# Spectral rows for the inverse transform gathered one token block at a time instead of eight

## The chip, the core and the metric

The kernel runs on one core of a Trainium2 chip. A core has five engines that work side by side, each through its own queue in the order in which the instructions were written into it: PE (TensorE, matrix multiplication into PSUM; the profile counts its weight loads apart, as PEld), DVE (VectorE), ACT (ScalarE), POOL (GpSimd) and SP (SyncE, which here only issues DMAs). SBUF is the working memory, PSUM holds what PE accumulates. The metric is the device time of one execution in microseconds (us), lower is better. Shapes are given as partitions x elements per partition.

## The reference

The input x has 2048 tokens of 448 features (f32). With LN for a layer normalisation over the features, the reference computes

```
xn  = LN(x)
A   = irfft2(rfft2(xn, axes=(token, feature)) * (w_r + 1j*w_i))
h   = gelu(LN(xn) @ w1); quarters of the features shifted by +1, -1, +2, -2 tokens
x1  = xn + shifted(h) @ w2
B   = x1 + gelu(LN(x1) @ w3) @ w4
out = x + A + B
```

w1 and w2 are 448 x 448, w3 is 448 x 1792, w4 is 1792 x 448, and w_r and w_i are 2048 x 225. The spectral branch A has four steps that matter here: a real transform over features and over part of the tokens, a transform over the rest of the tokens, the product with the weights, and the way back. The change lies at the beginning of the way back.

## The kernel before

**Tiling.** Token number 16a + b is row a of block b, so there are 16 blocks of 128 tokens, one token per partition; xb(b) is the f32 tile part of block b in xt. It first holds the normalised input, then everything that is added to it. Every f32 operand of a matmul is split into two f16 parts, high and low, and each product is made of three passes (high x high, high x low, low x high), the tuple PASS in the code.

**Stages in the order of the program.** Loads, the first normalisation, w1, the shifts and w2 (`w1_unit`, `w2_tile`); the second normalisation (`ln2`); the MLP with w3 and w4 for pairs of blocks, G = 0 to 7, each in seven steps fp (`front` makes 256 hidden features of a pair and their gelu, `back` multiplies them with w4); beside it the forward transform (`step1`) and, for 16 chunks of frequencies c, the spectral product (`chunk_a`, `chunk_b`, `chunk_z`, `chunk_c`); last the inverse stage for 16 blocks (`gather_u`, `inv_a`, `inv_b`, `finish`).

**Around the change.** `chunk_c` writes, for one chunk c, both f16 parts of its spectral rows into Y (L641 on ACT, L642 on DVE). Y is one tile of [128, 2 parts, 4 families q, 16 chunks c, 128]; the view Y1 reads the last 128 as 16 blocks b of 8 rows k. An inverse matmul for block b needs, as its weights, 128 columns: the 8 rows k of all 16 chunks c. In Y these stand in 16 runs of 8 elements, 128 elements apart. `gather_u` copies them on DVE (L651) into a tile U in which they are contiguous. As every block needs a row of every chunk, no gather can begin before the last `chunk_c` is through.

`gather_u(b0)` takes eight blocks at a time: two tiles (high and low part) of [128, 4, 8, 128] f16, one buffer each, and eight copies of 113 x 1024 elements, one for each part and each q. The first call serves blocks 8 to 15, the second blocks 0 to 7. The second writes the same two buffers and so waits until all inverse matmuls of the first eight blocks have read them.

`inv_a(b)` then runs 12 matmuls of 113 columns (L659) into a PSUM bank pe (tag "tr", two banks), copies it out with a scale on ACT (L663), folds it with two additions on POOL (L666, L667) and four additions and subtractions on DVE (L668 to L671) into v, and splits v into vh (L673 on ACT, L674 on DVE). The work tile of L663 to L671 alternates between two stage buffers; vh has two. `inv_b(b)` runs three matmuls of 448 columns (L681) into a PSUM bank py (tag "sp", two banks), and adds the result to xb(b) on DVE (L682). `finish(b)` loads the block's original x into one of two rows xr, adds xb(b) to it (L493 on DVE) and stores it. Blocks are taken in the order 12 to 15, 8 to 11, 0 to 7. Blocks 12 to 15 are finished later, in the MLP of the last two pairs.

**What sets the order.** Nothing here is ordered by hand. A planner simulates the engines with durations of its own and writes each engine's queue beforehand, taking among the instructions that are ready the one of the best priority. Priorities follow the order of the program, with two exceptions: the MLP's matmuls (`front` L381, `back` L716) have the priority FILL, below everything else, and what empties their PSUM banks (the gelu L694 and the split L696 on ACT, L697 on DVE, and the additions L728 and L723 on DVE) has EVAC, above everything else. So the matmuls of the MLP fill PE where the spectral branch leaves it free. `mlp(range(3, 6))` stands ahead of the inverse stage in the program, and `mlp(range(6, 8), last=True)` behind it. Both add to xb(b), and additions to one xb(b) keep the order of the program.

Of the kernel before, what the change touches and what calls it, by code (L numbers as in the profile page):

```python
# [13 lines left out]
F16 = mybir.dt.float16  # L14
# [6 lines left out]
NB, NC = 16, 16  # L21
# [98 lines left out]
def body(tc, nc, x, wf, w1, w2, w3, w4, c_g, c_n, c_small, out):  # L120
    V, A, P, T, SY = nc.vector, nc.scalar, nc.gpsimd, nc.tensor, nc.sync
# [13 lines left out]
    def pool(name, bufs=1, side="left", space=None):  # L135
        kw = dict(name=name, bufs=bufs, reuse_waits="tile")
        if space is not None:
            kw["space"] = space
        else:
            kw["side"] = side  # L140
        cm = tc.tile_pool(**kw)
        opened[name] = cm
        return cm.__enter__()
# [6 lines left out]
    def bank(tag, name):  # L150
        return ps.tile([128, 512], F32, tag=tag, bufs=2, name=name)
# [16 lines left out]
    def stage(name, n, side, dtype=F32):  # L168
        t = pw.tile([128, 1808], F32, tag=f"stage{side}", bufs=1, name=name)
        return (t if dtype is F32 else t.bitcast(dtype))[:, :n]  # L170
# [325 lines left out]
    def finish(b):  # L496
        SY.dma_start(ov[:, b], unscaled(b))
# [146 lines left out]

    U, vhs = {}, {}

    def gather_u(b0):
        U[b0] = [pv.tile([128, 4, 8, 128], F16, tag=f"U{p}", bufs=1, name=f"U{b0}{p}") for p in range(2)]
        for p in range(2):
            for q in range(4):  # L650
                V.tensor_copy(out=U[b0][p][:113, q].rearrange("p b (c k) -> p b c k", c=NC),  # L651
                              in_=Y1[:113, p, q, :, b0:b0 + 8].rearrange("p c b k -> p b c k"))

    def inv_a(b):
        pe = bank("tr", f"pe{b}")
        for q in range(4):
            kd = 113 - q // 2
            for n, (ui, ii) in enumerate(PASS):
                T.matmul(pe[:, 113 * q:113 * q + 113], U[b // 8 * 8][ui][:kd, q, b % 8, :],  # L659
                         cI[ii][:kd, 113 * q:113 * q + 113], start=n == 0, stop=n == 2)  # L660
        w = stage(f"e{b}", 1808, b % 2)
        e, v = w[:, 0:452], w[:, 904:904 + D]
        A.activation(out=e, in_=pe[:, :452], func=AF.Copy, scale=VPRE)  # L663
        u = w[:, 452:904].rearrange("p (a b d) -> p a b d", a=2, b=2)
        uf = u.rearrange("p a b d -> p a (b d)")
        P.tensor_tensor(out=uf[:, 0], in0=e[:, 0:226], in1=e[:, 226:452], op=ALU.add)  # L666
        P.tensor_tensor(out=uf[:, 1], in0=e[:, 0:226], in1=e[:, 226:452], op=ALU.subtract)  # L667
        V.tensor_tensor(out=v[:, 0:113], in0=u[:, 0, 0], in1=u[:, 0, 1], op=ALU.add)  # L668
        V.tensor_tensor(out=v[:, 447:335:-1], in0=u[:, 0, 0, 1:113], in1=u[:, 0, 1, 1:113], op=ALU.subtract)
        V.tensor_tensor(out=v[:, 224:112:-1], in0=u[:, 1, 0, 0:112], in1=u[:, 1, 1, 0:112], op=ALU.subtract)  # L670
        V.tensor_tensor(out=v[:, 225:336], in0=u[:, 1, 0, 1:112], in1=u[:, 1, 1, 1:112], op=ALU.add)  # L671
        vh = pv.tile([128, 2, D], F16, tag="vh", bufs=2, name=f"vh{b}")
        A.activation(out=vh[:, 0], in_=v, func=AF.Copy)  # L673
        V.tensor_tensor(out=vh[:, 1], in0=v, in1=vh[:, 0], op=ALU.subtract)  # L674
        vhs[b] = vh

    def inv_b(b):
        vh = vhs.pop(b)
        py = bank("sp", f"py{b}")
        for n, (vi, ri) in enumerate(PASS):  # L680
            T.matmul(py[:, :D], cV[ri], vh[:, vi], start=n == 0, stop=n == 2)  # L681
        V.scalar_tensor_tensor(out=xb(b), in0=py[:, :D], scalar=sc[:, 1:2], in1=xb(b), op0=ALU.mult, op1=ALU.add)  # L682
# [209 lines left out]
    Y1 = Y.rearrange("p i q c (b k) -> p i q c b k", k=8)  # L892
# [33 lines left out]
    pv = pool("pv", side="right")  # L926
    bs = [*range(12, 16), *range(8, 12), *range(8)]
    for n in range(17):
        if n in (0, 8):
            gather_u(8 - n)  # L930
        if n < 16:
            inv_a(bs[n])
        if n:
            b = bs[n - 1]
            inv_b(b)
            if b < 12:
                finish(b)
# [27 lines left out]
```

## Time and profile before

| | |
|---|---|
| time, median of 3 runs | 420.48 us (420.2 to 420.87) |
| the profiled execution's own time | 420.4 us |
| busy: PEld | 291.7 us |
| busy: DVE | 291.6 us |
| busy: ACT | 248.1 us |
| busy: POOL | 118.6 us |
| first and last copy of a gather begin at | 286.2 and 312.5 us |
| first and last inverse matmul (L659) begin at | 289.3 and 355.0 us |
| DMA, whole span | 47.61 MB |

The profile is that of one execution; times in it count from the start of its span. A row of the timeline gives start, duration, engine, line, operation, output <- inputs, shape, and the number of instructions merged into it; in square brackets stands for how long the engine had been idle before it and which instruction ended that wait. A row of a window view gives the stretch, its length, an engine's busy time with the number of its instructions, the granted clock of PE as a share of full speed, and two figures for DMA. "PEld" rows are weight loads, which run beside matmuls. The end of a matmul is modelled, and consecutive ones overlap, so their spacing is read from their starts.

### The profile page before, as it was taken

What the parts mean: (1) busy time and instruction counts of PE and PEld (TensorE: products, weight loads), DVE (VectorE), ACT (ScalarE), POOL (GpSimd) and SP (SyncE); (2) the same over time, 40 slices, a digit from 0 to 9 for tenths busy, and PEclk for the clock granted to TensorE, in tenths of its full rate; (3) what the DMA queues carried; (4) which work ended last, traced back from release to release, by engine and by line L of the source; (5) the groups of instructions that cost most, each with busy time, mean ns of one, the idle gap of its engine ahead of it and who ended that gap; (6) DMA issues with size and microseconds to landing.
All of it is one profiled execution on the core that took longest, in us unless ns stands there. A gap on an engine that the chain in (4) does not pass through costs nothing.

```text
span 418.6 us, 8535 instructions
## 1 busy us (share of the span) xinstructions
PE 409.8 (98%) x3329; PEld 291.7 (70%) x3329; DVE 291.6 (70%) x615; ACT 248.1 (59%) x428; POOL 118.6 (28%) x204
## 2 busy tenths in 40 slices
PE   7999999999999999999999999999999999999996
PEld 3655555765668777776887887777776767577785
DVE  4888899798774766652689889865999529942112
ACT  4698869972758866632678888864534414422331
POOL 3876700101345746300031221211454203200000
DMA  8959982734761365315056555610001003331001
GB/s 271 362 174 175 275 174 95 132 78 90 191 156 50 89 234 165 93 41 140 14 142 173 149 144 142 177 39 2 2 2 68 22 2 132 134 133 40 5 0 45
DMA packets 51832, 47.61 MB, mean 114 GB/s; under 512 B 33936, under 2 KB 47056, under 8 KB 51792
## 3 DMA queue, kind: packets, MB, share of 16 engines
q1 hardware_dynamic: 51792, 47.07, 41.7%
q8 instruction: 26, 0.43, 0.4%
q14 instruction: 14, 0.11, 0.1%
HBM read 35.52 MB, written 3.67 MB: 94 GB/s over the span
## 4 chain that ended last, share of the span: by engine, by line
PE 72%; DVE 14%; DMA 6%; issue 5%; POOL 1%; ACT 1%; SPq 1%; POOLq 0%; DVEq 0%
PE pw L381 25%; PE acc L716 22%; PE pw L450 7%; PE pw L410 6%; PE ps L536 3%; PE pu L638 2%; PE pp L593 2%; PE px L610 2%; DMA xr<-x 1%; DVE w4p L265 1%; DMA out<-xr 1%; PE pta L370 1%; DMA x2mem<-y 1%; DVE xt L682 1%; DVE sta L289 1%
## 5 line engine op out<-in xcount | busy, mean ns | idle before, releaser
L381 PE MATMUL pw<-x2mem,w3p 128*128 128x256 f16 x1232 | 151.8, 273 | 0.0
L716 PE MATMUL acc<-w4p,hf 128*128 128x448 f16 (+1 forms) x714 | 140.0, 341 | 0.7 <-DVE hf L697 0.7
L381 PEld LDWEIGHTS <-w3p 128*128 128x128 f16 x1232 | 118.9, 98 | 23.1 <-issue 0.9
L716 PEld LDWEIGHTS <-hf 128*128 128x128 f16 x714 | 69.2, 98 | 49.2 <-DVE hf L697 1.6
L697 DVE SCALAR_TENSOR_TENSOR hf<-pw,h,hf 128x512 f16<-128x512 f32 x56 | 41.7, 747 | 55.5 <-ACT hf L696 55.3
L694 ACT ACTIVATE pw<-pw,pe 128x512 f32<-128x512 f32 x56 | 36.6, 655 | 70.5 <-PE pw L381 69.4
L450 PE MATMUL pw<-w2p,h 112*128 112x448 f16 x192 | 40.1, 352 | 0.8 <-DMA h<-hs 0.8
L696 ACT ACTIVATE hf<-pw,h 128x512 f16<-128x512 f32 x56 | 38.3, 686 | 1.4
L619 POOL TENSOR_TENSOR z<-te 128x450 f32<-128x450 f32 x16 | 16.3, 1016 | 74.0 <-DVE te L617 74.0
L410 PE MATMUL pw<-w1p,xT 128*128 128x448 f16 x176 | 35.3, 352 | 0.0
L450 PEld LDWEIGHTS <-h 112*128 112x128 f16 x192 | 18.7, 98 | 17.0 <-DMA h<-hs 1.0
L666 POOL TENSOR_TENSOR e<-e 128x226 f32<-128x226 f32 x16 | 13.9, 866 | 56.5 <-ACT e L663 45.3
L410 PEld LDWEIGHTS <-xT 128*128 128x128 f16 x176 | 16.9, 98 | 16.2 <-DVE xT L375 0.8
L600 ACT ACTIVATE pf<-pp 64x450 f16<-64x450 f32 x32 | 17.3, 540 | 16.7 <-DVE pf L601 8.2
L601 DVE TENSOR_TENSOR pf<-pp,pf 64x450 f16<-64x450 f32 x32 | 19.9, 622 | 5.3 <-ACT pf L600 5.0
L663 ACT ACTIVATE e<-pe 128x452 f32<-128x452 f32 x16 | 8.7, 547 | 15.6 <-DVE vh L674 12.3
L516 POOL TENSOR_TENSOR xr<-xf 128x452 f32<-128x452 f32 x8 | 9.7, 1208 | 28.3 <-issue 22.9
L615 ACT ACTIVATE te<-px 64x450 f32<-64x450 f32 x32 | 17.2, 538 | 0.5
L673 ACT ACTIVATE vh<-e 128x448 f16<-128x448 f32 x16 | 9.2, 574 | 14.0 <-DVE e L671 8.3
L519 POOL TENSOR_TENSOR f<-xr 128x452 f32<-128x452 f32 x16 | 16.1, 1028 | 0.6
L527 DVE TENSOR_TENSOR xh<-f,xh 128x452 f16<-128x452 f32 x16 | 11.8, 780 | 5.9 <-ACT xh L526 5.9
L681 PE MATMUL py<-vh,csm 128*128 128x448 f16 x48 | 13.5, 352 | 1.5 <-DVE vh L674 0.7
(163 smaller groups left out, 602.8 us busy)
## 6 DMA issues: line engine op xcount, KB each, us to landing
wc<-wf SPq DMA_DIRECT2D x32, 225.0 KB, 3.7
wl<-wf SPq DMA_DIRECT2D x8, 450.0 KB, 3.7
xt<-x SPq DMA_DIRECT2D x8, 448.0 KB, 8.2
xf<-x SPq DMA_DIRECT2D x8, 448.0 KB, 3.7
w3raw<-w SPq DMA_DIRECT2D x3, 896.0 KB, 12.8
xr<-x SPq DMA_DIRECT2D x12, 224.0 KB, 2.6
out<-xr SPq DMA_DIRECT2D x12, 224.0 KB, 2.0
gn<-c_g SPq DMA_DIRECT2D x16, 128.0 KB, 3.3
```

The costliest lines, as they stand in the source:

```text
L381: T.matmul(ps_out, wp[:, wi + t, cols], xT[:, xi + t, tok], start=t == 0 and wi + xi == 0, stop=t == 3 and wi == 4)
L410: T.matmul(pm[:, :D], xTs[g][:, xi + t, 128 * i:128 * i + 128], w1p[:, wi + t], start=t == 0 and p == 0, stop=t == 3 and p == 2)
L450: T.matmul(pm[:, :D], hT[g][:112, 4 * hi + k, o:o + 128], w2p[:, wi, k], start=n == 0, stop=n == 11)
L519: P.tensor_tensor(out=f[:, :, k:k + 2].rearrange("p b s d -> p s b d"), in0=u[:, :, 0], in1=u[:, :, 1], op=op)
L600: A.activation(out=hi, in_=src, func=AF.Copy)
L601: V.tensor_tensor(out=lo, in0=src, in1=hi, op=ALU.subtract)
L615: A.activation(out=e[64 * h:64 * h + 64], in_=px_[64 - 64 * h:128 - 64 * h, :2 * DF], func=AF.Copy)
L619: P.tensor_tensor(out=z, in0=t[:, 0], in1=t[:, 1], op=ALU.add)
L694: A.activation(out=pm, in_=pm, func=AF.Gelu_apprx_tanh, scale=r3)
L696: i = A.activation(out=h[:, 0], in_=pm, func=AF.Copy, scale=h3)
L697: j = V.scalar_tensor_tensor(out=h[:, 1], in0=pm, scalar=h3, in1=h[:, 0], op0=ALU.mult, op1=ALU.subtract)
L716: m = T.matmul(to, h[:, hi, o:o + 128], w4p[0][:, wi, f, r], start=f == 0 and n == 0, stop=f == 13 and n == 2)
```

## The change

A gather now serves one block. `gather_u(b)` makes one tile U of [128, 2 parts, 4 families, 128] f16, in a ring of four buffers, and fills it with two copies of 113 x 512 elements, one for each part, each over all four families. That is 32 copies in place of 16, with the same elements in all. `inv_a(b)` takes its weights from that tile, with the same shapes as before. In the loop the first two blocks are gathered ahead of the first `inv_a`, and then each time the next block ahead of the present one's `inv_a`. The buffers take 4 x 2 KB per partition in place of 2 x 8 KB.

```diff
-    def gather_u(b0):
-        U[b0] = [pv.tile([128, 4, 8, 128], F16, tag=f"U{p}", bufs=1, name=f"U{b0}{p}") for p in range(2)]
+    def gather_u(b):
+        U[b] = pv.tile([128, 2, 4, 128], F16, tag="U", bufs=4, name=f"U{b}")
         for p in range(2):
-            for q in range(4):
-                V.tensor_copy(out=U[b0][p][:113, q].rearrange("p b (c k) -> p b c k", c=NC),
-                              in_=Y1[:113, p, q, :, b0:b0 + 8].rearrange("p c b k -> p b c k"))
+            V.tensor_copy(out=U[b][:113, p].rearrange("p q (c k) -> p q c k", c=NC), in_=Y1[:113, p, :, :, b])
 
     def inv_a(b):
         pe = bank("tr", f"pe{b}")
+        u = U.pop(b)
         for q in range(4):
             kd = 113 - q // 2
             for n, (ui, ii) in enumerate(PASS):
-                T.matmul(pe[:, 113 * q:113 * q + 113], U[b // 8 * 8][ui][:kd, q, b % 8, :],
+                T.matmul(pe[:, 113 * q:113 * q + 113], u[:kd, ui, q],
                          cI[ii][:kd, 113 * q:113 * q + 113], start=n == 0, stop=n == 2)
@@
     for n in range(17):
-        if n in (0, 8):
-            gather_u(8 - n)
+        if n == 0:
+            gather_u(bs[0])
+        if n < 15:
+            gather_u(bs[n + 1])
         if n < 16:
             inv_a(bs[n])
```

## The prediction

> **What bounds the kernel now.** First the page: its span, and the busy share of each engine. PE is the matrix engine, DVE the vector engine, ACT the scalar engine, POOL the general one.
>
> ```profile
> span 418.6 us, 8535 instructions
> PE 409.8 (98%) x3329; PEld 291.7 (70%) x3329; DVE 291.6 (70%) x615; ACT 248.1 (59%) x428; POOL 118.6 (28%) x204
> ```
>
> PE is busy for 409.8 of 418.6 us. The profiled execution took 420.4 us, so 1.8 us lie around the span, and it stands 0.08 us under the median of 420.48 us. Whatever the change does, it must do it to PE's few idle microseconds, since the matmuls stay the same in number and shape. So the second view is PE's busy time by stretch (stretch, length, busy time, granted clock), from the first gather copy on.
>
> ```profile
> 286.00:331.00 45.00, 43.70 (x406) 1.00 0.06 22
> 345.00:366.00 21.00, 20.47 (x157) 1.00 0.39 132
> 366.00:411.00 45.00, 45.00 (x362) 1.00 0.12 42
> ```
>
> The reader is to see that after 366 us PE is never idle: there only MLP matmuls are left. In the inverse stage the page sees 45.00 - 43.70 = 1.30 and 21.00 - 20.47 = 0.53 us, 1.83 us in all. A matmul's shown end is modelled and overlaps the next, so short gaps hide in busy time. Starts show them. In a stretch of pure MLP work PE's timeline has:
>
> ```profile
> 331.45 2.56 PE L381 MATMUL pw<-x2mem,w3p 128*128 128x256 f16 x22
> 333.85 2.43 PE L716 MATMUL acc<-w4p,hf 128*128 128x448 f16 x12
> 336.12 2.57 PE L381 MATMUL pw<-x2mem,w3p 128*128 128x256 f16 x22
> ```
>
> From start to start, 22 matmuls of 256 columns take 2.40 us, 0.109 each, and 12 of 448 columns take 2.27 us, 0.189 each. By columns, one of 113 takes 113/256 of 0.109, an estimate of 0.048. With these the stall at the second gather is read from the timeline of all engines:
>
> ```profile
> 309.59 3.76 POOL L666 TENSOR_TENSOR e<-e 128x226 f32<-128x226 f32 x1 [3.81 <-ACT e L663]
> ...
> 310.15 2.76 DVE L651 COPY U<-y 113x1024 f16<-113x1024 f16 x8
> ...
> 312.17 1.02 PE L659 MATMUL pe<-csm,U 113*128 113x113 f16 x10
> 312.63 0.17 PEld L659 LDWEIGHTS <-U 112*128 112x128 f16 x3 [0.15 <-DVE U L651]
> ...
> 313.03 1.04 PE L381 MATMUL pw<-x2mem,w3p 128*128 128x256 f16 x8
> ...
> 313.76 1.00 DVE L674 TENSOR_TENSOR vh<-e,vh 128x448 f16<-128x448 f32 x1
> ...
> 314.81 0.35 PE L681 MATMUL py<-vh,csm 128*128 128x448 f16 x1 [0.74 <-DVE vh L674]
> ```
>
> Eight copies hold DVE for 2.76 us. The ten L659 matmuls, which read what the copies write, take 313.03 - 312.17 = 0.86 us where 10 x 0.048 = 0.48 would do: 0.38 us lost, and the weight load names the copy. The eight L381 matmuls then take 314.81 - 313.03 = 1.78 us where 8 x 0.109 = 0.87 would do: 0.91 us lost, until L681 gets its vh from the L674 that stood behind the copies on DVE. So **1.29 us of PE time is lost at the second gather.** The other stall of size is late in the stage:
>
> ```profile
> 361.85 0.54 PE L716 MATMUL acc<-w4p,hf 128*128 128x448 f16 x2
> 362.70 1.12 PE L716 MATMUL acc<-w4p,hf 128*128 128x448 f16 x5 [0.32 <-DVE hf L697]
> 364.04 0.55 PE L681 MATMUL py<-vh,csm 128*128 128x448 f16 x2 [0.21 <-DVE xt L682]
> ```
>
> Here 0.85 - 2 x 0.189 = 0.47 and 1.34 - 5 x 0.189 = 0.39, together 0.86 us, wait for DVE work that is no gather.
>
> **The change part by part.** It removes 16 copies of 1024 elements a partition and adds 32 of 512; no DMA, matmul, ACT or POOL instruction is added or taken, and SP's queue gets nothing new. The copies' price, with the nearest row for one that has no length (a copy of one element), and the group in the stretch of the stage:
>
> ```profile
> L651 DVE COPY U<-y x16: 412/416/422, 286.2 to 312.5; 113x1024 f16<-113x1024 f16 x16
> L565 DVE COPY wt<-wpb x1: 159/159/159, 200.5 to 200.5; 128x1 f32<-128x1 f32 x1
> L651 DVE COPY U<-y 113x1024 f16<-113x1024 f16 x16 | 5.5, 417 | 0.0
> ...
> L668 DVE TENSOR_TENSOR e<-e 128x113 f32<-128x113 f32 x12 | 5.1, 423 | 3.2 <-POOL e L666 3.2
> L671 DVE TENSOR_TENSOR e<-e 128x111 f32<-128x111 f32 x12 | 4.3, 359 | 0.0
> ```
>
> (The first two give minimum, median and maximum in ns; the others total busy us and mean ns.) No copy of 512 elements is in the trace. If nothing of a copy were fixed it would take 208 ns, if everything were, 416. I take the one-element row as the fixed part: 159 + (416 - 159)/2 = 288 ns. Sixteen copies are busy for 5.5 us, 0.344 each, so consecutive ones overlap by 0.07 us. The new ones then hold DVE for 32 x (0.288 - 0.07) = 7.0 us, 1.5 us more than now; the ends are 32 x 0.138 = 4.4 (1.1 us less) and 32 x 0.346 = 11.1 us (5.6 more). [...]
>
> **The first gather.** Now:
>
> ```profile
> 286.18 2.77 DVE L651 COPY U<-y 113x1024 f16<-113x1024 f16 x8
> 288.86 0.75 DVE L697 SCALAR_TENSOR_TENSOR hf<-pw,h,hf 128x512 f16<-128x512 f32 x1
> 291.84 0.64 DVE L668 TENSOR_TENSOR e<-e 128x113 f32<-128x113 f32 x1 [2.23 <-POOL e L666]
> ```
>
> With the change the first block's rows are there after two copies, 2 x 0.22 = 0.44 us, so the first inverse block can start 2.77 - 0.44 = 2.3 us sooner, and the copies of the next three blocks (1.3 us) fit under the 2.23 us for which DVE now waits on POOL. What that gains at the end is **nothing**: PE shows no wait for this burst, MLP matmuls cover it, and what is pulled forward of the inverse pushes as much MLP work behind it. If that cover were gone, it would be worth the 2.3 us. The reason why it cannot be carried on is this pair of DVE's rows:
>
> ```profile
> 344.26 1.44 DVE L728 SCALAR_TENSOR_TENSOR xt<-acc,p,xt 128x448 f32<-128x448 f32 x2 [3.37 <-PE acc L716]
> 345.62 1.27 DVE L682 SCALAR_TENSOR_TENSOR xt<-py,sc,xt 128x448 f32<-128x448 f32 x2
> ```
>
> L682 of blocks 10 and 11 adds to the same xt as L728 of MLP pair 5 and comes after it in the program, so the inverse stops until the third group of MLP work is through, however early it began.
>
> **The second gather** goes: its copies come in pairs, up to three blocks ahead, as ring slots come free. That takes away the 0.38 and the 0.91 us, as far as nothing else makes vh late at that place. Next in line there is the work that stood around the burst on DVE, of 0.6 to 1.0 us an instruction, so I take off the whole 1.29 and keep 0 as the other end.
>
> **The added wait.** Copy n must wait until the 12 L659 matmuls of block n - 4 have read its slot, and behind it on DVE stand L668 to L674, L682 and the MLP's L697, on which PE's L716 waits. Now only the second burst has such a wait, for all eight blocks. A slot is needed again three blocks later, so I price it at nothing; PE's order hides it, and without that cover a pair could cost what the weight load shows at 312.63 us, 0.15 us, 12 times: 1.8 us.
>
> **The copies beside POOL.** At 309.59 us POOL's L666 took 3.76 us, with all eight copies inside. DVE's two-input adds meet POOL too; the first row gives one add over the whole run, the others DVE and POOL in the stretch:
>
> ```profile
> L668 DVE TENSOR_TENSOR e<-e x16: 257/266/656, 291.8 to 362.6; 128x113 f32<-128x113 f32 x16
> 286.00:331.00 45.00, 39.37 (x96) 1.00 0.06 22
> 286.00:331.00 45.00, 18.52 (x24) 1.00 0.06 22
> ```
>
> An undisturbed add takes 0.266 us, the slowest 0.656, so one meeting costs DVE up to 0.39 us. DVE is 39.37/45 = 87% busy and POOL 18.52/45 = 41%. Eight of the new copies fall before POOL has inverse work; if the other 24 meet it by its busy share and wait each time, that is 24 x 0.39 x 0.41 = 3.8 us; with the 1.5 us of fixed parts DVE comes 5.3 us later over the stage, and in the other direction POOL gets its 3.2 us at L666 back. What does DVE's lateness cost PE? L668 and L671 already lose 12 x (0.423 - 0.266) + 12 x (0.359 - 0.266) = 3.0 us to such meetings, and PE's idle time beside the burst is 1.30 - 0.74 = 0.56 us: at most 0.19 us of PE per us of DVE. So the cost lies between 0 and 5.3 x 0.19 = 1.0 us; a DVE that falls fully behind would pass on all of it, which is the rival below. I take the 1.5 us alone, 0.3 us, since POOL's meetings are given back at L666.
>
> [...]
>
> **Sum:** 420.4 - 1.29 + 0.3 = 419.4 us; with the ends of the cost (0 to 1.0) 419.1 to 420.1.
>
> **The rivals.** *Slower: DVE falls behind among POOL's work.* PE takes its instructions in the written order, so if MLP matmuls stand behind L681 and vh is late, PE stands still. For it: DVE is 87% busy, and both stalls shown above are waits for DVE. Against it: 0.19 us per us so far. If half of the 5.3 us reaches PE, it is 420.4 - 1.29 + 2.65 = 421.8 us; if all, 424.4. It is slower than before once more than 1.29/5.3 = 24% of DVE's lateness arrives at PE.
>
> *No difference: the stall moves.* Both the order on PE and that on DVE are laid out anew from the first gather on, since each block's copies are free at other times. Then L681 may wait for vh at another place, as it does at 364.04 us, where no gather is near. The 1.29 us come back elsewhere: 420.4 us.
>
> *Much faster: the early start clears the stage.* With 2.3 us of lead and no gap between blocks 11 and 0, DVE's work is spread and the 0.86 us at 362 us goes too: 420.4 - 1.29 - 0.86 = 418.3 us; and all idle time of the page is 1.83 us, so it can hardly be much more. Against it: the later stretch begins at the same L728 as now.
>
> *The change does not do what it says:* if no slot is free in time, the copies come as late as now, with the 1.8 us of the added wait on top and the 1.29 us kept: 422.2 us. Against it: with four slots the planner may copy three blocks ahead.
>
> **How the numbers follow.** Forecast 0.42, of which 0.30 is faster and 0.12 within the bound (419.4 is only 1.1 us under the median); much faster 0.12; no difference 0.12; slower by DVE's lateness 0.28; slots too late 0.06. A measurement of this kernel can tell about 0.2%, 0.84 us, from no change: faster is under 419.64 us, slower over 421.32. So faster 0.42, same 0.24, slower 0.34. The forecast's own range is 419.1 to 420.1 us. The range for 8 in 10 goes from 418.2, just under the much faster case, to 422.4, over the half-lateness and late-slot cases; the full lateness of 424.4 is left out.
>
> **What would show it.** If the steps are right, the first L659 stands about 2.3 us earlier than its copies now allow; copies come in pairs of about 0.29 us each; no L666 takes over 1.7 us; PE's idle time up to 331 us falls from 1.30 to about 0.5 us, and that after 366 us stays zero. The price is wrong if a copy takes near 0.21 or 0.42 us, the hiding is wrong if weight loads at L659 wait for copies, and the slower rival is right if L651 copies of 0.6 us and more stand ahead of waits of L681 or L716 for DVE. The whole argument is wrong if PE idles after 366 us, or if the instructions ahead of the first gather change place.

## The result and the profile after

The changed kernel takes 421.44 us (median of 16 runs, 421.11 to 421.75), the kernel before 420.56 us (16 runs). The ratio is 1.0023, 95% interval 1.0017 to 1.0030: **slower by 0.9 us** (0.7 to 1.3). 419.4 us and "faster" were forecast.

The page of the changed kernel, and PE's busy time by stretch (stretch, length, busy time, clock, DMA):

```profile
span 419.8 us, 8553 instructions
PE 410.8 (98%) x3329; PEld 291.6 (69%) x3329; DVE 292.6 (70%) x631; ACT 248.1 (59%) x428; POOL 115.5 (28%) x204
```

```profile
286.00:331.00 45.00, 42.79 (x403) 1.00 0.07 22
345.00:366.00 21.00, 20.54 (x156) 1.00 0.40 132
366.00:411.00 45.00, 45.00 (x359) 1.00 0.12 42
```

PE's idle time up to 331 us rose from 1.30 to 2.21 us. These 0.91 us are the whole difference; the later stretch (0.46 in place of 0.53) and the time after 366 us (none) did not move. The profiled pair is 1.2 us apart, but 0.3 us of that lies ahead of the gather: the last L642 begins at 285.89 here and at 285.57 in the kernel before, as in these two rows of the two timelines.

```profile
285.89 0.69 DVE L642 SCALAR_TENSOR_TENSOR y<-pu,y 113x512 f16<-113x512 f32 x1 [1.87 <-ACT y L641]
```

```profile
285.57 0.69 DVE L642 SCALAR_TENSOR_TENSOR y<-pu,y 113x512 f16<-113x512 f32 x1 [1.89 <-ACT y L641]
```

From here on, lines behind 650 have a number one lower in the changed kernel: the copy is L650, the inverse matmuls L658, POOL's additions L665 and L666, the fold L667 to L670, vh L672 and L673, the block's second matmuls L680.

What PE waited for up to 331 us (total, times, longest, in us), in the kernel before and then in the changed one:

```profile
PE py L681 <- DVE vh L674: 0.7, 1, 0.7
PE py L681 <- ACT vh L673: 0.5, 2, 0.3
```

```profile
PE py L680 <- DVE vh L673: 1.0, 1, 1.0
PE py L680 <- ACT vh L672: 0.7, 1, 0.7
PE py L680 <- DVE xt L681: 0.2, 1, 0.2
PE pe L658 <- ACT e L662: 0.2, 1, 0.2
```

Two stalls hold most of the loss, and each stands where the kernel before lost time too. The first, in the timeline of all engines:

```profile
298.76 0.59 POOL L665 TENSOR_TENSOR e<-e 128x226 f32<-128x226 f32 x1 [1.83 <-ACT e L662]
...
298.91 0.57 DVE L669 TENSOR_TENSOR e<-e 128x112 f32<-128x112 f32 x1
299.30 0.62 POOL L666 TENSOR_TENSOR e<-e 128x226 f32<-128x226 f32 x1
...
299.40 0.65 DVE L670 TENSOR_TENSOR e<-e 128x111 f32<-128x111 f32 x1
299.44 0.60 PE L381 MATMUL pw<-x2mem,w3p 128*128 128x256 f16 x4
...
300.15 0.58 ACT L672 ACTIVATE vh<-e 128x448 f16<-128x448 f32 x1 [1.47 <-DVE e L670]
...
300.78 0.54 PE L680 MATMUL py<-vh,csm 128*128 128x448 f16 x2 [0.74 <-ACT vh L672]
```

The reader is to see a meeting: DVE finishes one block's fold (L669, L670) while POOL adds for the next one (L665, L666). The two DVE instructions take 0.57 and 0.65 us where an undisturbed one takes 0.26; so ACT makes vh 0.7 us later than it could, and PE, whose four L381 matmuls (300.78 - 299.44 = 1.34 us for 4 x 0.109 = 0.44) are all that was written ahead of L680, stands still for 0.90 us. At the same place the kernel before lost about 0.5 us, there too behind a fold that met POOL (two of its instructions take 0.66 and 0.65 us). The second:

```profile
310.42 0.57 ACT L672 ACTIVATE vh<-e 128x448 f16<-128x448 f32 x1
...
310.75 1.18 DVE L650 COPY U<-y 113x512 f16<-113x512 f16 x2
...
311.14 0.64 POOL L666 TENSOR_TENSOR e<-e 128x226 f32<-128x226 f32 x1
...
311.85 0.67 DVE L493 SCALAR_TENSOR_TENSOR x2mem<-xt,s,x2mem 128x448 f32<-128x448 f32 x1
...
312.45 0.48 DVE L650 COPY U<-y 113x512 f16<-113x512 f16 x2
...
312.60 0.49 PE L381 MATMUL pw<-x2mem,w3p 128*128 128x256 f16 x3
...
312.85 0.67 DVE L493 SCALAR_TENSOR_TENSOR x2mem<-xt,s,x2mem 128x448 f32<-128x448 f32 x1
313.45 0.61 DVE L673 TENSOR_TENSOR vh<-e,vh 128x448 f16<-128x448 f32 x1
...
314.11 0.35 PE L680 MATMUL py<-vh,csm 128*128 128x448 f16 x1 [1.02 <-DVE vh L673]
```

This is the stall that the change was to remove. ACT's half of vh was there at 310.99 us, but on DVE four copies and two L493 are written ahead of L673, and the first two copies take 1.18 us beside POOL where the next two take 0.48. PE loses 314.11 - 312.60 - 3 x 0.109 = 1.18 us, against 0.91 in the kernel before.

So these two places cost 2.1 us now; in the kernel before they cost about 1.8, the 0.38 us at L659 included. The rest of the difference lies in smaller waits. By starts, the changed kernel has three that are new: 0.39 us before the L680 at 309.02 and 0.21 before that at 316.11, both spent waiting for L681, and 0.33 before the L658 at 323.92, waiting for L662. One of 0.4 us at 320.60 in the kernel before is gone. By starts that makes about 2.2 us before and 3.0 after. The window view shows less, as a matmul's shown end hides short gaps, but the difference is the same within 0.1 us.

The copies as a row over the whole run, as a group up to 331 us, and where the first of them stand:

```profile
L650 DVE COPY U<-y x32: 275/284/690, 286.5 to 327.5; 113x512 f16<-113x512 f16 x32
```

```profile
L650 DVE COPY U<-y 113x512 f16<-113x512 f16 x32 | 9.2, 337 | 1.6 <-PE pe L658 1.6
```

```profile
286.50 1.70 DVE L650 COPY U<-y 113x512 f16<-113x512 f16 x8
...
289.51 1.39 PE L658 MATMUL pe<-csm,U 113*128 113x113 f16 x24
...
290.42 1.41 DVE L650 COPY U<-y 113x512 f16<-113x512 f16 x4 [1.57 <-PE pe L658]
```

An undisturbed copy takes 0.284 us; the mean is 0.337, so 32 x (0.337 - 0.284) = 1.7 us went to meetings with POOL. The first eight, in a row, run at 1.70/8 = 0.21 us each, while POOL is idle (its first addition begins at 291.10 us).

### The profile page after: what moved, and what is told of

Read it like the earlier page. It is cut to its first block, busy times and chain, and to the rows that moved or that the text cites. A ratio compares the mean times of both kernels' runs of the same rounds, so it can differ in the third digit from the quotient of the medians.

```text
span 419.8 us, 8553 instructions
## 1 busy us (share of the span) xinstructions
PE 410.8 (98%) x3329; PEld 291.6 (69%) x3329; DVE 292.6 (70%) x631; ACT 248.1 (59%) x428; POOL 115.5 (28%) x204
## 4 chain that ended last, share of the span: by engine, by line
PE 66%; DVE 18%; DMA 6%; ACT 5%; issue 2%; POOL 1%; SPq 1%; ACTq 0%; POOLq 0%; DVEq 0%
PE pw L381 24%; PE acc L715 23%; PE pw L410 4%; PE pw L450 3%; PE pu L638 3%; PE ps L536 3%; PE pp L593 2%; PE px L610 2%; DVE hf L696 2%; DMA x2mem<-y 2%; ACT w3p L264 2%; DVE w4p L265 2%; DMA xr<-x 1%; DVE U L650 1%; DVE y L484 1%
## 5 line engine op out<-in xcount | busy, mean ns | idle before, releaser
L381 PE MATMUL pw<-x2mem,w3p 128*128 128x256 f16 x1232 | 152.1, 273 | 0.0
L381 PEld LDWEIGHTS <-w3p 128*128 128x128 f16 x1232 | 119.0, 98 | 23.6 <-issue 1.2
L665 POOL TENSOR_TENSOR e<-e 128x226 f32<-128x226 f32 x16 | 12.5, 783 | 60.6 <-ACT e L662 49.9
L672 ACT ACTIVATE vh<-e 128x448 f16<-128x448 f32 x16 | 9.2, 574 | 14.9 <-DVE e L670 12.8
L662 ACT ACTIVATE e<-pe 128x452 f32<-128x452 f32 x16 | 8.7, 547 | 15.5 <-DVE vh L673 12.8
L527 DVE TENSOR_TENSOR xh<-f,xh 128x452 f16<-128x452 f32 x16 | 12.7, 832 | 5.9 <-ACT xh L526 5.9
L680 PE MATMUL py<-vh,csm 128*128 128x448 f16 x48 | 13.7, 353 | 2.3 <-DVE vh L673 1.0
```

The source lines that it names most:

```text
L381: T.matmul(ps_out, wp[:, wi + t, cols], xT[:, xi + t, tok], start=t == 0 and wi + xi == 0, stop=t == 3 and wi == 4)
```

## The experiments

Theories, in the order in which they came. *Lateness*: DVE has more to do, and PE pays 0.24 us for each us of it. *Place*: the copies are written ahead of vh work. *Meetings*: DVE and POOL hold each other up, which makes vh later than the order written on PE allows. *Order* (called chance in most of the expectations): which meetings hurt is an accident of the order that the planner lays out; against it *price*, a fixed cost of the short spread copies. *Depth*: the ring's size decides. All times are medians, the ratio is to the kernel before on the same chip, and "idle" is PE's idle time from 286 to 331 us by the window view of the one profiled execution.

| run | us | ratio (95% interval) | idle, us |
|---|---|---|---|
| before | 420.56 | 1 | 1.30 |
| changed | 421.44 | 1.0023 (1.0017 to 1.0030) | 2.21 |
| e1_half | 421.67 | 1.0023 (1.0013 to 1.0033) | 2.56 |
| e2_shape | 419.53 | 0.9974 (0.9964 to 0.9984) | 0.83 |
| e8_late | 421.60 | 1.0020 (1.0011 to 1.0030) | 2.23 |
| e3_act | 419.64 | 0.9979 (0.9970 to 0.9989) | 1.14 |
| e7_nopool_after | 418.11 | 0.9940 (0.9928 to 0.9953) | 0.00 |
| e7_nopool_before | 418.00 | 0.9939 (0.9926 to 0.9951) | 0.00 |
| e6_pairs | 420.16 | 0.9993 (0.9984 to 1.0002) | 0.93 |
| e9_ring8 | 419.77 | 0.9985 (0.9977 to 0.9994) | 0.87 |
| e11_actcopy_after | 418.91 | 0.9950 (0.9937 to 0.9962) | 0.00 |
| e9_ring2 | 420.48 | 0.9992 (0.9983 to 1.0001) | 1.44 |
| e14_ring6 | 421.26 | 1.0020 (1.0011 to 1.0029) | 1.98 |
| e12_best | 417.92 | 0.9930 (0.9918 to 0.9943) | 0.00 |
| p1_vh3_before | 421.58 | 1.0040 (1.0027 to 1.0053) | 1.98 |
| p1_vh3_after | 422.87 | 1.0063 (1.0051 to 1.0076) | 3.42 |
| p2_swap_before | 420.07 | 0.9992 (0.9978 to 1.0005) | 1.30 |
| p2_swap_after | 421.32 | 1.0029 (1.0018 to 1.0041) | 2.20 |
| e15_four_act | 421.03 | 1.0014 (1.0005 to 1.0023) | 2.17 |
| e13_dveadds | 418.16 | 0.9944 (0.9931 to 0.9956) | 0.00 |

Read down the last column first: the time rises and falls with PE's idle time in this one stretch, whatever was edited. It moves by more than the column says: the five runs at 0.00 are 1.8 to 2.8 us faster than the kernel before on their chip, since the view leaves out short gaps and the wait near 362 us is gone from three of them too.

**Half of the copies (e1_half).** Expected: 

> Leaves out the copies of the low parts (the second pass reads the high part in their place), so 16 copies of 512 in place of 32, everything else as in the changed kernel. Lateness theory (PE stands still because DVE's queue in the inverse stage takes longer: 9.2 us of copies in place of 5.5, and PE lost 0.9 us for these 3.7 us, 0.24 per us): copies of 4.6 us, 421.4 - 0.24 x 4.6 = 420.3 us, PE's idle time up to 331 us near 1.3 us in place of 2.2. Place theory (it is the copies planned ahead of the vh work on DVE, not their sum): half as much in the way, 420.9 us. Chance theory (any new order moves the time by up to 1 us either way): no relation to DVE's time.

```diff
-        for p in range(2):
+        for p in range(1):
             V.tensor_copy(out=U[b][:113, p]...
-    u[:kd, ui, q]
+    u[:kd, 0, q]
```

PE's and then DVE's busy time up to 331 us:

```profile
286.00:331.00 45.00, 42.44 (x402) 1.00 0.07 22
```

```profile
286.00:331.00 45.00, 37.29 (x95) 1.00 0.07 22
```

DVE has 3.2 us less to do than in the changed kernel (40.49) and 2.1 less than before (39.37), and PE idles more. Lateness falls: the sum of DVE's work is not what PE pays for.

**Only the shape (e2_shape).** Expected: 

> The kernel before with its two gathers of eight blocks, but each as 16 copies of 512 elements in place of 8 of 1024: only the shape of the copies changes, not their time. Lateness theory: DVE is busy with copies for about 7.0 us in place of 5.5, without meeting POOL more often; 420.5 + 0.24 x 1.5 = 420.9 us. Place theory: the second burst is 0.75 us longer and PE waits for it, the first is hidden; 421.2 us. Chance theory: 419.6 to 421.6.

```diff
-            for q in range(4):
-                V.tensor_copy(out=U[b0][p][:113, q]..., in_=Y1[:113, p, q, :, b0:b0 + 8]...)
+            for i in range(8):
+                V.tensor_copy(out=U[b0][p][:113, :, i].rearrange("p q (c k) -> p q c k", c=NC),
+                              in_=Y1[:113, p, :, :, b0 + i])
```

419.53 us, faster than both. So the 32 short copies by themselves are not the cost, and neither lateness (420.9) nor place (421.2) had it.

**Later gathers (e8_late).** Expected: 

> The changed kernel with each block's gather written directly ahead of its own inv_a, not one block ahead; ring of four as it was. Place theory: the copies stand behind more of the earlier block's work on DVE, PE loses less for vh: 420.6 us or less. Lateness theory: the same copies, 421.4 us. Chance theory: 420.4 to 422.4.

```diff
-        if n == 0:
-            gather_u(bs[0])
-        if n < 15:
-            gather_u(bs[n + 1])
+        if n < 16:
+            gather_u(bs[n])
```

421.60 us, with the two stalls unmoved (0.9 and 1.2 us lost, at 299.8 and 313.0 us). Place, in the sense of when the gather is written, did not have it.

**Copies on ACT (e3_act).** Expected: 

> The changed kernel with all 32 copies on ACT in place of DVE. Lateness theory: DVE has 9.2 us less to do and no copy meets POOL; 421.4 - 0.24 x 9.2 = 419.2 us, as far as ACT, which is busy for less than half of the stage, has room for 32 x 0.6 = 19 us. Place theory: the copies now stand ahead of L662 and L672 on ACT, so 420 to 421 us. If ACT becomes the limit: over 421.4 us with waits for ACT at L680.

```diff
-            V.tensor_copy(out=U[b]..., in_=Y1[:113, p, :, :, b])
+            A.activation(out=U[b]..., in_=Y1[:113, p, :, :, b], func=AF.Copy)
```

419.64 us: 1.8 us under the changed kernel, less than lateness asked for. Neither stall is at its old place; PE still idles for 1.14 us, waiting at other blocks for vh (0.8 us) and for L681 (0.4 us).

**No POOL (e7_nopool_after, e7_nopool_before).** Expected: 

> The changed kernel without POOL's two additions L665 and L666 in the inverse stage: DVE's four operations read e directly, so the fold is incomplete. No POOL instruction is left in the stage that DVE could meet. New theory, meetings: the order on PE is planned without the 0.39 us by which DVE's two-input adds and copies wait for POOL, so vh comes later than planned and PE stands still at L680. Then PE loses at most 0.7 us up to 331 us in place of 3.2, and the time is about 421.4 - 2.5 = 418.9 us, the same as for the kernel before treated alike. Chance theory (planned order alone): PE still loses 1.5 to 3.5 us, 419.8 to 421.8 us. Lateness theory is already doubtful, as half of the copies were taken away without gain; it would say 421.4 - 0.24 x 6.2 = 419.9 us.

 And: 

> The kernel before without POOL's two additions in the inverse stage, the fold incomplete in the same way. Meetings: PE loses at most 0.7 us up to 331 us in place of 2.3; 420.6 - 1.6 = 419.0 us, within 0.4 us of the changed kernel without them. Chance theory: a difference of about 1 us between the two stays, with either sign. If the second burst by itself is a price, 0.4 to 1.3 us of it stays at the second gather.

```diff
-        P.tensor_tensor(out=uf[:, 0], in0=e[:, 0:226], in1=e[:, 226:452], op=ALU.add)
-        P.tensor_tensor(out=uf[:, 1], in0=e[:, 0:226], in1=e[:, 226:452], op=ALU.subtract)
-        u = w[:, 452:904]...
-        uf = ...
+        u = w[:, 0:452]...
```

PE's busy time up to 331 us, first the changed kernel so treated, then the kernel before:

```profile
286.00:331.00 45.00, 45.00 (x425) 1.00 0.06 22
```

```profile
286.00:331.00 45.00, 45.00 (x425) 1.00 0.07 22
```

No idle time in either, and the two kernels are equal (418.11 and 418.00 us; intervals overlap). With POOL's additions goes the loss, and with the loss the difference between the two gathers. The second burst alone, still in the second kernel (its 16 copies take 0.416 to 0.423 us each, the last begins at 309.5 us), costs PE nothing.

**Chain or meetings (e11_actcopy_after).** Expected: 

> The changed kernel with POOL's two additions L665 and L666 replaced by two plain copies of the same 226 columns on ACT, so the fold is incomplete but the chain from pe to vh keeps two steps at that place, and POOL does nothing. It separates two readings of the run without the additions, in which PE lost only 0.1 us up to 331 us. Meetings: what matters is that DVE no longer waits for POOL; PE loses under 0.7 us again, 418.0 to 418.7 us. Shorter chain: what mattered was that a step of some 1.2 us was gone; with two ACT steps in its place PE loses 2 us or more, 420.0 us or over.

```diff
-        P.tensor_tensor(out=uf[:, 0], ..., op=ALU.add)
-        P.tensor_tensor(out=uf[:, 1], ..., op=ALU.subtract)
+        A.activation(out=uf[:, 0], in_=e[:, 0:226], func=AF.Copy)
+        A.activation(out=uf[:, 1], in_=e[:, 226:452], func=AF.Copy)
```

No idle time again; 418.91 us, a little above the expected range but far from 420. The chain from pe to vh kept its two steps, so a missing step is not why the loss went. The steps are shorter, though: ACT is busy for 28.23 us up to 331 us with 61 instructions, in the changed kernel for 19.80 with 35, which is 0.32 us for each one more, and POOL's additions have medians of 0.60 and 0.61. This run alone does not exclude that a shorter chain helped.

**The ring's depth and the size of a piece (e9_ring2, e14_ring6, e9_ring8, e6_pairs).** Expected: 

> The changed kernel with a ring of two tiles, so a block's copies must wait until the matmuls two blocks back have read their slot. Depth theory (the nearer a copy must stand to its use, the more it is among other DVE work): 421.4 to 422.2 us, with waits of L658 for the copies. Chance theory with meetings (the planned order decides which meetings fall where PE has no slack): anything from 419.6 to 421.8 us.

 

> The changed kernel with a ring of six tiles. Depth theory: between four (421.4) and eight (419.8), so 420.2 to 421.0 us. Chance theory with meetings: no order by depth, anything from 419.6 to 421.8 us.

 

> The changed kernel with a ring of eight tiles: the copies of the first eight blocks can all run at once at the start of the stage, those of the last eight as slots come free. If spreading costs: about half of the spread copies are left, 420.5 us. If only the burst at the start is good and the second may be spread: 419.6 us, as for the kernel with 32 short copies in two bursts (419.5 us). Chance theory: 419.6 to 421.8 us.

 

> Blocks gathered two at a time, two copies of 1024 elements for each pair, in a ring of two tiles: 16 copies as before the change, spread over the stage as after it. If spreading costs (each copy has its own chance to meet POOL and stands between other work on DVE): 421 to 422 us, PE loses 3 us or more up to 331 us. If the number of copies costs (the fixed part of each): 420.5 us. Chance theory: 419.6 to 421.8 us.

```diff
-    tag="U", bufs=4
+    tag="U", bufs=2        (and 6, and 8)
```

```diff
+        t = pv.tile([128, 2, 2, 4, 128], F16, tag="U", bufs=2, name=f"U{b}")
...
+            V.tensor_copy(out=t[:113, p].rearrange("p b q (c k) -> p b (q c) k", c=NC),
+                          in_=Y1[:113, p, :, :, b:b + 2].rearrange("p q c b k -> p b (q c) k"))
...
+        if n < 14 and n % 2 == 0:
+            gather_u(bs[n + 2])
```

Two, four, six and eight tiles give 420.48, 421.44, 421.26 and 419.77 us: no order by depth, so depth falls. Pairs of blocks, spread as much, are at 420.16. Spreading by itself is no price either.

**Two small changes in both kernels (p1, p2).** Expected: 

> The kernel before with three vh buffers in place of two: a small change beside the gather, which makes the planner lay the inverse stage out anew. Only the comparison with the changed kernel treated alike counts. Price theory (spread short copies cost 0.9 us in themselves): 0.9 us under the changed kernel with three buffers. Order theory (which of the meetings with POOL fall where PE has no work written in front of L680 is an accident of the order): the difference has another size or sign; either kernel between 419.5 and 421.7 us.

 

> The changed kernel with three vh buffers. Price theory: 0.9 us (0.5 to 1.3) over the kernel before treated alike. Order theory: a difference of another size or sign, between 419.5 and 421.7 us.

 

> The kernel before with the two blocks of every pair taken in the opposite order in the inverse stage (13, 12, 15, 14 and so on), the same work. Price theory: 0.9 us under the changed kernel treated alike. Order theory: another size or sign of the difference; 419.5 to 421.7 us.

 

> The changed kernel with the two blocks of every pair taken in the opposite order. Price theory: 0.9 us (0.5 to 1.3) over the kernel before treated alike. Order theory: another size or sign of the difference; 419.5 to 421.7 us.

```diff
-    tag="vh", bufs=2
+    tag="vh", bufs=3
```

```diff
-    bs = [*range(12, 16), *range(8, 12), *range(8)]
+    bs = [b ^ 1 for b in (*range(12, 16), *range(8, 12), *range(8))]
```

The differences are 1.29 and 1.25 us (421.58 to 422.87, 420.07 to 421.32), of the same sign as the 0.88 us and inside the 0.5 to 1.3 us that the price theory gave; 422.87 lies outside what the order theory gave. This looks like a price, but it settles less than was hoped: in both changed kernels the two stalls stand at 299 and 312 us as before, with the same losses to 0.1 us, and in both kernels before theirs do. The small edits did not reach the order of the first 40 us of the stage; the swap, by its stalls, is the same order measured again. With three vh buffers both kernels have one more stall, at 329 us (0.83 us before, 1.31 after).

**The copies at the two stalls (e15_four_act).** Expected: 

> The changed kernel with the copies of four blocks (10, 11, 2 and 3) on ACT, the other twelve blocks' on DVE as they were. These are the copies that stand ahead of the vh work at the changed kernel's two large stalls (299.4 and 312.6 us), and that took 0.62 and 0.70 us longer there beside POOL. If those copies make these two stalls: both stalls fall below 0.4 us, PE loses about 1.3 us less, 420.1 us. If the stalls belong to the fold's meetings alone: they stay, 421.4 us, with waits of L672 for the fold.

```diff
+            o, i = U[b]..., Y1[:113, p, :, :, b]
+            if b in (10, 11, 2, 3):
+                A.activation(out=o, in_=i, func=AF.Copy)
+            else:
                 V.tensor_copy(out=o, in_=i)
```

PE's longest waits from 286 to 366 us (total, times, longest; L684 is this kernel's L680, L662 its L658):

```profile
PE py L684 <- ACT vh L676: 0.9, 1, 0.9
PE pe L662 <- ACT e L666: 0.9, 1, 0.9
PE py L684 <- DVE vh L677: 0.4, 1, 0.4
```

The two stalls are gone from their places, and two of 1.06 and 1.02 us stand at 301.6 and 321.4 us in their stead, with a third of 0.58 us that ends at 315.78; 421.03 us. The copies took part in the stalls that they stood at, but taking them away moved the loss and hardly made it smaller.

**Full work without meetings (e12_best, e13_dveadds).** Expected: 

> Full work, without POOL in the inverse stage: its two additions run on DVE, and the 32 copies of the changed kernel on ACT. DVE loses 9.2 us of copies and all meetings (6.2 us) and gains 32 additions of 226 columns, about 0.31 us each, 10 us. Meetings: PE loses under 0.7 us up to 331 us, 418.2 to 418.8 us, faster than both kernels. If ACT's 32 copies of 0.6 us make vh late: 419.6 us, as with the copies on ACT alone (419.6).

 

> Full work: POOL's two additions on DVE, the copies on DVE too. No meetings are left, but DVE has the most to do of all kernels, about 34.7 + 10 = 44.7 us of the 45 us up to 331 us. Meetings: the planner knows this work, so PE loses under 0.7 us up to 331 us, and the time is 418.0 to 419.0 us. Lateness: DVE is full, PE waits for it; over 420 us.

```diff
-        P.tensor_tensor(out=uf[:, 0], ...
-        P.tensor_tensor(out=uf[:, 1], ...
+        V.tensor_tensor(out=uf[:, 0], ...
+        V.tensor_tensor(out=uf[:, 1], ...
```

e13_dveadds is this edit in the changed kernel; e12_best has the copies on ACT beside it. PE's and DVE's busy time up to 331 us in e13_dveadds:

```profile
286.00:331.00 45.00, 45.00 (x425) 1.00 0.07 22
```

```profile
286.00:331.00 45.00, 41.51 (x136) 1.00 0.07 22
```

DVE is as busy as in any run of the table (40.49 in the changed kernel), with the same 32 spread copies, and PE never waits there: 418.16 us. e12_best, at 417.92 us, is the fastest with all its work; the two can't be told apart. Both beat the kernel before by 0.6 to 0.7%. This is the plainest evidence against lateness and against a price of the copies, and for meetings. Two limits: DVE was expected to be busy for 44.7 us and was for 41.51, so the test of a full DVE is weaker than planned, and the two additions take 0.39 us each on DVE, so here too the chain is shorter than with POOL.

## Why the prediction was wrong, step by step

**What bounds the kernel: right.** PE's idle time in this stage is all that a change here can move; it moved by 0.91 us, the time by 0.88, and nothing happened after 366 us. Its size was read too small: by starts the kernel before loses about 2.2 us up to 331 us. Only the second gather was counted; the stalls of 0.5 us at 299.81 and 0.4 us at 320.60, the two waits for ACT's vh in the list above, were left out. So the 1.83 us that were called all the idle time are no bound, and the runs without POOL gain up to 2.8 us.

**The price of a copy: right.** 0.288 us was forecast, 0.284 measured; 0.22 in a burst was forecast, 0.21 measured.

**The first gather: right in its worth, wrong in its detail.** It brought nothing. But the first inverse matmul did not come 2.3 us sooner: it begins at 289.51, with the 0.3 us of offset at the same time as before (289.3), since it stands on PE behind much the same MLP matmuls. The copies were done at 288.2 us.

**The second gather: the step that failed.** "I take off the whole 1.29" put the stall at 313 us down to the burst. The 0.38 us did go: no weight load of L658 waits for a copy any more. The 0.91 us did not: at the same L680 there are now 1.18 us. The rows of the kernel before, between the burst and L681, show why:

```profile
312.83 1.00 DVE L493 SCALAR_TENSOR_TENSOR x2mem<-xt,s,x2mem 128x448 f32<-128x448 f32 x1
313.32 0.96 POOL L667 TENSOR_TENSOR e<-e 128x226 f32<-128x226 f32 x1
```

This L493 and the L674 behind it, which the prediction shows, take 1.00 us each, where in the changed kernel L493 and L673 at that place take 0.67 and 0.61. So 0.33 + 0.39 = 0.72 of the 0.91 us is an estimate of what the meetings with POOL cost there, and little is left for the length of the burst itself; POOL's addition stood there because the one before it had lasted through the burst (3.76 us in place of 0.58). In the changed kernel the first two copies meet POOL instead and lose 0.70 us. The burst was the work that stood ahead of vh at that moment, not the reason why PE had no slack there; with a burst of the same length and no POOL (e7_nopool_before) PE lost nothing, though in an order laid out anew. The other end that was kept for this term, no gain, is what happened: other work on DVE (four copies, two L493) stands there now.

**The copies beside POOL: the meetings were seen, their measure was wrong.** The prediction added up DVE's lateness and charged PE 0.19 us per us. Measured, the copies lost 1.7 us to POOL (0 to 3.8 were forecast, 0 was taken), and POOL's longest addition still took 1.81 us, over the 1.7 that was to be its limit; but PE pays by the single meeting that falls on a chain with little work written ahead of L680, 0.7 us in the first stall, and pays nothing for DVE's sum: half of the copies changed nothing, a fuller DVE without meetings (41.51 us in place of 40.49) cost nothing. So the fixed parts (1.5 us more DVE work) that were taken as the cost are the part that costs nothing.

**Spread copies and bursts.** The copies lost 1.7 us to POOL when spread and almost nothing in the two bursts of the kernel before (the longest of 16 took 0.422 us there, the median 0.416). That spreading therefore must cost does not follow: e9_ring2, e9_ring8 and e6_pairs spread copies too and are not slower than before, though the copies of e9_ring2 lose as much to POOL as those of the changed kernel (mean 0.342 us).

**The added wait: right.** The copies at 290.42 us waited 1.57 us for the matmuls of the block four back, with no idle time of PE up to 300 us (14.00 of 14.00 us).

**The rivals.** "Slower: DVE falls behind among POOL's work" was the right side, with 421.8 us against 421.44, and vh waits at L680 as its sign; its measure (half of 5.3 us) was that of the failed step. That 421.8 lies so near is luck: it takes off 1.29 us, of which 0.91 did not go, and adds 2.65 us for a sum of DVE work that costs nothing. "The stall moves" describes what e15_four_act shows.

**What stays open.** Shown: with POOL out of the stage, PE's loss up to 331 us is zero in all five runs and the difference between the two gathers is gone; and at the large stalls of both kernels DVE's instructions beside POOL take 0.7 to 0.8 us longer than undisturbed ones. Not excluded: that a shorter chain helped in the five runs, or that the planner reckoned with too short a time for POOL's additions themselves. Against that being the main part, DVE is not idle ahead of the two large stalls of the changed kernel; it is its instructions that are longer. Not settled: why the order with a ring of four (and two variants near it, and six) puts the meetings where PE idles for 2 to 2.6 us and that of the eight-block gather where it idles for 1.3 (with two vh buffers; 1.98 with three). Every edit makes the planner lay out the rest anew, so no run here changed the meetings with the order held fixed, and a rule by which one could have foretold the sign was not found. That the planner's durations leave the meetings out fits the runs without POOL, in which PE has no idle time up to 331 us, but no run shows it directly.

## What to carry to other kernels

When PE is nearly full and its order is written beforehand, a stall at a burst need not be the burst's: look for instructions of one form that take two different times (here 0.26 and 0.65 us), and take their excess off the stall before booking it on the burst. If two engines hold each other up in a stage, moving one's work to the other can win even when the other is nearly full: DVE at 41.5 of 45 us without POOL beat every kernel that shared the stage. And a change that makes a planner lay out a stage anew should be forecast with a spread from the stage's whole idle time, on both sides, before a gain is booked.

## What the runs showed of the hardware

A meeting of DVE and POOL shows in the durations of both. Where POOL's additions are under way, DVE's additions of the fold take up to 0.66 us in place of 0.26, and a single copy takes up to 0.690 us in place of 0.284. With no POOL instruction in the stage the longest copy takes 0.293 us (e7_nopool_after) and 0.294 (e13_dveadds), and the fold's four additions 0.27 us in the mean (e13_dveadds). In the kernel before, from 312.83 us on, an L493, POOL's L667 and an L674 overlap one after the other and take 1.00, 0.96 and 1.00 us in place of 0.67, 0.58 and 0.61. One POOL addition can also last as long as a whole run of DVE work: 3.76 us beside an L493 and eight copies in the kernel before, and in the changed kernel 1.81 us beside an L493, two copies and an L673:

```profile
303.09 1.81 POOL L665 TENSOR_TENSOR e<-e 128x226 f32<-128x226 f32 x1 [3.17 <-ACT e L662]
```

By what means the two slow each other these runs do not show. ACT's copies of the same rows take 0.616 us each (median of e3_act; the longest of 32 takes 0.647), so none of them is lengthened as DVE's are.
